# Output stores and turned transfers move one place back in the DMA queue, and the output tile gets six buffers

## Chip, cores and metric

The kernel runs on one core of one Trainium2 chip. The metric is device time in microseconds (us), the median of several runs.

## What is computed

Two layers in a row: attention with a relative position bias, and a mixture of eight low-rank adapters on its output.

```python
# q, k, v: (8 batches, 8 heads, 576, 64); bias_table: (32, 8)
scores = q @ k.T / sqrt(64) + bias_table[bucket(|i - j|)]   # per head
attn   = exp(scores - max) / (sum + 1e-9)
x      = (attn @ v)  ->  (4608 rows, 512)                   # heads side by side
logits = x @ w_gate                                         # 8 experts
topk   = the two largest; w = softmax over the two
out    = x + sum over the two of w_e * (x @ A[e]) @ B[e]    # A: 512x16, B: 16x512
```

Each batch gives 576 output rows: 512 from the main part and 64 from the tail.

## The kernel before, in words

**The pairs.** The work goes in 32 steps, one for each pair of heads of a batch: `u` counts them, batch `b = u // 4`, pair `hp = u % 4` (loop at L747). The order of the instructions on each engine is the order of the code, written out by hand. A pair's step has these parts:

- At the top, the SyncE queue issues loads: the tail of the next batch when `hp` is 0 (L754), `q` and `k` of pair `u + 4` (L758) and `v` of pair `u + 3` (L763). That is five loads a pair: one of `q`, two of `k`, two of `v`, 256 KB for each of the three.
- GpSimd casts `q` and `k` of pair `u + 2` and `v` of pair `u` to bf16 (`prep`, L722, with the casts at L137 and L141) and multiplies edge terms (L430, L432).
- TensorE makes four score tiles (`keys`, L368: L376 and L381) and ScalarE takes the exponential of each (L387), plus one for the edges of the next pair (L424). There are three score tiles in PSUM.
- TensorE multiplies the probabilities of the pair before with its values (L440, L450, L464), and VectorE divides by the sums (L508, L521). The results go to `xn`, and to `xe` for the 64 tail rows of two batches.
- TensorE transposes `q` and `k` of the next pair (L317), and VectorE copies the result (L321).

**The adapters.** Their work on a finished batch is spread over the next pairs by `moe` (L634), which enters each part in tables by pair number; the loop runs each table's entries at its place. A batch has two groups of two tiles of 128 rows, and each two batches have a group of one tile for the tail rows (`group`, L608). A group's parts, in order:

- Its rows have to be turned (transposed) into `xT`. Some tiles go through TensorE (L348, with a copy at L352; from batch 5 on L317 also), and the others through a turned transfer of the DMA, issued from SyncE: `send_x` (L355, issue at L357). The tables `send` and `sendx` hold these; `send` is run in the middle of a pair (L819), `sendx` at its end (L868). There are nine such transfers, and two more for the last batch (`send_last`, L360). `xT` has four buffers.
- Two to five pairs later, the gate matmuls read `xT` (`moe_z`, L539, matmul at L541), inside the group of matmuls of the values.
- Gate values follow on VectorE, ScalarE and GpSimd (L555 to L578), and a transposition on TensorE (L586).
- `moe_d` (L591) multiplies by `B` (L593) and adds `x` on VectorE into the tile `ot` (L596). `ot` belongs to the pool `ms`, which has three buffers for each tag. Each group has one buffer of two tiles, and each tile is stored as soon as it is done (L617, or L605 for tail rows). `moe_d` runs from the tables `dl2` (L816, L827) and `dls` (L847).

**The queue.** Nearly all DMAs are issued by SyncE, one after another: a transfer whose data is not ready holds all behind it. So the order in which the code issues loads, turned transfers and stores is the order in which they start. In the kernel before, a pair's queue is: loads, then the stores and turned transfers that come up in that pair.

**The end.** After the last pair, the last batch's adapters run by themselves (from L902), with their own stores (L1079, L1082, L1009).

Of the kernel before, what the change touches and what calls it, by code (L numbers as in the profile page):

```python
# [10 lines left out]
FP32 = mybir.dt.float32  # L11
# [26 lines left out]
def kernel(  # L38
# [14 lines left out]
    Dm = H * D  # L53
# [21 lines left out]
    ms = ctx.enter_context(tc.tile_pool(name="moe_sb", bufs=3))  # L75
# [15 lines left out]
    NU = len(units)  # L91
# [11 lines left out]
    def load(u, names="qkv", eng=nc.sync):  # L103
        b, hp = units[u]
        for nm in names:
            src = {"q": q, "k": k, "v": v}[nm]
            t = stg.tile([128, 2, 4 * D], FP32, name=f"{nm}s", tag=f"{nm}s")
            heads = src[b, 2 * hp:2 * hp + 2, :SM, :]
            if nm != "q":
                for h in range(2):  # L110
                    eng.dma_start(out=t[:, h, :].rearrange("p (g x) -> p g x", g=2),
                                      in_=heads[h].rearrange("(g p c) d -> p g (c d)", g=2, c=2))
            else:
                eng.dma_start(out=t, in_=heads.rearrange("h (p c) d -> p h (c d)", c=4))
            stage[(u, nm)] = t
# [425 lines left out]
            nc.tensor.matmul(zl, lhsT=gr.xT[:, t, c, :], rhs=AW[:, c, :], start=(first and c == 0),  # L541
                             stop=(c == 3), skip_group_check=True)

    left = []

    def moe_zc(gr, t, zl):
        if gr.z is None:
# [43 lines left out]
    def moe_d(gr, t):  # L591
        dl = mp.tile([128, Dm], FP32, name="dl", tag="mm")
        nc.tensor.matmul(dl, lhsT=gr.zT[:, t, :], rhs=Bc, start=True, stop=True)  # L593
        if gr.ot is None:
            gr.ot = ms.tile([128, len(gr.x), Dm], FP32, name="ot", tag="ot")
        nc.vector.tensor_tensor(gr.ot[:, t, :], dl, gr.x[t], op=ALU.add)  # L596
        gr.left -= 1
        if gr.solo:
            gr.store(gr.ot[:, t:t + 1, :], t)
        elif not gr.left:  # L600
            gr.store(gr.ot)

    def store_tail(b, ot, engs=(nc.sync, nc.sync)):
        for o in range(2):
            engs[o].dma_start(out=out[(b + o) * S + SM:(b + o + 1) * S, :],  # L605
                              in_=ot[64 * o:64 * o + 64, :])

    def group(b, i):  # L608
        gr = Group()
        gr.zT_ps, gr.z, gr.zT, gr.ot, gr.solo = {}, None, None, None, False  # L610
        if i < 2:
            gr.x = [xs[b][:, c, :] for c in (2 * i, 2 * i + 1)]
            gr.flat = xs[b][:, 2 * i:2 * i + 2, :].rearrange("p c d -> p (c d)")

            def store(ot, t=0):
                c, n = TILES[2 * i + t], ot.shape[1]
                nc.sync.dma_start(out=out[b * S:b * S + SM, :].rearrange("(p c) n -> p c n", c=4)  # L617
                                  [:, c:c + 2 * n - 1:2, :], in_=ot)
        else:
            gr.x = [xe[b // 2]]  # L620
            gr.flat = xe[b // 2]

            def store(ot, t=0):
                store_tail(b - 1, ot[:, 0, :])
        gr.store, gr.left = store, len(gr.x)
        return gr

    gate1, gates, xts, zs, zts, dls, send, sendx, xas, dl2 = ({} for _ in range(10))

    def at(where, u, *item):  # L630
        where.setdefault(u, []).append(item)


    def moe(b, u):  # L634
        g0, g1 = group(b, 0), group(b, 1)
        tiles = ((g0, 0), (g0, 1), (g1, 0), (g1, 1))
        k = B - 3 - b
        odd = b % 2
        for i in range(1 if odd else 3):
            if k >= 0:  # L640
                at(xas, u + 1 + i, *tiles[i])
        if k < 0:
            for i in range(4):
                at(xts, u + i // 2, *tiles[i])
        else:
            if k == 0:
                at(xts, u + 1, *tiles[1])
            elif odd:
                at(send, u, send_x, g0, 1, 2)
            at(sendx, u, send_x, g1, 1 - odd, 2)  # L650
        uz = (2, 3, 4, 5) if k > 0 else (2, 2, 3, 3) if k == 0 else (1, 1, 2, 2)
        ug, ut = ((5, 6), (6, 7, 8, 9)) if k > 1 else ((4, 6), (5, 6, 7, 8)) if k > 0 else ((3, 4), (4, 5, 5, 6)) if k == 0 else \
            ((2, 3), (3, None, None, None))
        ud = ((dls, 6), (dls, 7), (dls, 8), (dl2 if k == 2 else dls, 9)) if k > 1 else \
            ((dls, 5), (dls, 6), (dls, 7), (dls, 8)) if k > 0 else \
            ((dl2, 5), (dls, 5), (dl2, 6), (dls, 6)) if k == 0 else ((dls, 3),)
        for i, (g, t) in enumerate(tiles):
            at(zs, u + uz[i], g, t)
            if ut[i] is None:
                left.append((g, t))  # L660
            else:
                at(zts, u + ut[i], g, t)
                at(ud[i][0], u + ud[i][1], moe_d, g, t)
        for i, g in enumerate((g0, g1)):
            at(gate1, u + ug[i], moe_w, g)
            g.late = u + ug[i] - 1 if k > 1 and not i else None
            g.solo = True
        if b % 2:
            gt = group(b, 2)
            o = k == 0  # L670
            if o:
                at(send, u + 1, send_x, gt, 0, 1)
            else:
                at(xas, u + 2, gt, 0)
            w = 3 if k > 1 else o
            gt.late = u + 3 + w if k > 1 else None
            at(zs, u + 3 + o, gt, 0)
            at(gate1, u + 4 + w, moe_w, gt)
            at(zts, u + 5 + w + (k > 1) + (k == 2), gt, 0)
            at(dl2, u + 6 + w + (k > 1), moe_d, gt, 0)  # L680
# [6 lines left out]
    t = Turn()  # L687
# [14 lines left out]
    t = Turn()  # L702
# [38 lines left out]
    def run(items):  # L741
        for fn, *args in items:
            fn(*args)
# [3 lines left out]
    for u in range(NU):  # L747
# [12 lines left out]
            load_tail(1)  # L760
        if u + 3 < NU:
            load(u + 3, "v")
        for c in KO[:2]:  # L763
            keys(u, c)
            keys_exp(u, c)
# [12 lines left out]
        if u:  # L778
            pa = pva.pop(u - 2, None)
            oa = 256 if xa or hp == 0 else (ER + E) * (len(zb) > 1)  # L780
            ia = (XO - oa) // 64

            def bank_b():
                pv = values_b(u - 1)
                zl = pv[:, 260:260 + ER + E]
                for gr, t in zb[:1]:
                    moe_z(gr, t, zl, False)
                o = 260 + (ER + E) * bool(zb)
                for i, (gr, t) in enumerate(ta[ia:]):
                    moe_t(gr, t, pv, o + i * 64)  # L790
                return pv, zl

            if pa is not None:
                for gr, t in xa:
                    turn_x(gr, t, pa)
                values_x(u - 2, pa)
                for i, (gr, t) in enumerate(ta[:ia]):
                    moe_t(gr, t, pa, oa + 64 * i)
                za = pa[:, :ER + E]
                for gr, t in zb[1:]:  # L800
                    moe_z(gr, t, za, True)
                for gr, t in xa:
                    copy_x(gr, t)
                for gr, t in ta[:ia]:
                    moe_tc(gr, t)
                normalise_x(u - 2, pa)
                for gr, t in zb[1:]:
                    moe_zc(gr, t, za)
            pv, zl = bank_b()
            for gr, t in ta[ia:]:  # L810
                moe_tc(gr, t)
            normalise_b(u - 1)
            for gr, t in zb[:1]:
                moe_zc(gr, t, zl)
            if u < 16:
                run(dl2.pop(u, []))  # L816
            if hp == 0:
                corners(pa[:, :256], b)
            run(send.pop(u, []))  # L819
        else:  # L820
            t = Turn()
            turn_tail(t, 0, 2)
            copy_tail(t, 0, 2)
            corners(mp.tile([128, 256], FP32, name="cps", tag="mm"), 0)
# [3 lines left out]
        if 0 < u < NU - 1:  # L828
            t = Turn()
# [9 lines left out]
            if xt:  # L839
                gr, c = xt[0]  # L840
# [4 lines left out]
        keys(u, KO[3])  # L845
        keys_exp(u, KO[3])
        run(dls.pop(u, []))  # L847
        if u in (4, 5):
            weights_turn(u - 4)
        if u == 0:  # L850
            factors_l()
            factors_t()
            corners_bias(0)
            edge_bias(0)
            prep(0)
        else:
            if hp == 0:
                corners_bias(b)
            values_a(u - 1)
            if u == NU - 1:  # L860
                values_x(u - 1, pva[u - 1])
            normalise_a(u - 1)
            if u == NU - 1:
                normalise_x(u - 1, pva[u - 1])
            for gr, i in zb:
                at(gates, gr.late or u, moe_g, gr, i)
            run(gates.pop(u, []))
            run(sendx.pop(u, []))  # L868
        if u < 3:
            cast(u + 2, "q", nc.vector)  # L870
        if u == 3:
# [251 lines left out]
```

## Time and profile before

| | us |
|---|---|
| median of 3 runs | 197.11 |
| lowest and highest | 196.76, 197.35 |
| the profiled execution | 194.04 |
| its span in the profile | 192.2 |
| ScalarE busy | 166.0 |
| TensorE busy | 167.9 |
| GpSimd busy | 138.5 |
| VectorE busy | 135.3 |

The span is the time from the first to the last instruction that the profiler has; the rest of the execution's time lies around it. TensorE's busy time says less than the others', because matmuls are pipelined and their ends are modelled. In the profile, PE is TensorE, DVE VectorE, ACT ScalarE, POOL GpSimd and SP SyncE; SPq is SyncE's sequencer, which issues DMAs. A row in a timeline has the start, the duration, the engine, the line, what is written and read, and in brackets the idle time of the engine just before it and what ended that. A row xN joins N instructions. The chain of waits has a start, a duration, and the work or the DMA that ended last at that point.

### The profile page before, as it was taken

To read this page: it belongs to the slowest core of one execution; us is meant where nothing else is said; L and a number is where in the kernel's file an instruction comes from. 1 tells how busy PE (TensorE), PEld (TensorE's weight loads), DVE (VectorE), ACT (ScalarE), POOL (GpSimd) and SP (SyncE) were. 2 spreads that over 40 slices of the span, in tenths; PEclk is the share of its full clock that TensorE was granted. 3 is DMA by queue.
4 is the path that set the end of the run, shared out by engine and by line. 5 is a ranking of instruction groups with operands and counts; after the bars stand their busy time and mean duration, and the time that the engine had idled before them with its cause. 6 is when DMAs were issued, how large, how long until landed. Compare 5 with 4: busy or idle time off the path is not lost.

```text
span 192.2 us, 11327 instructions
## 1 busy us (share of the span) xinstructions
PE 167.9 (87%) x4834; PEld 122.4 (64%) x4834; DVE 135.3 (70%) x460; ACT 166.0 (86%) x206; POOL 138.5 (72%) x286
## 2 busy tenths in 40 slices
PE   0458799999999998999999999997999939999970
PEld 0345466777777776777776777775766737766840
DVE  4510457666658976999799779997799657988760
ACT  3159999999999999999999999999889956899680
POOL 5195859877986998599979986696798959636030
PEclk9999999999999999999999999999999978999998
DMA  5689989897877898898789975967999999334366
GB/s 148 192 186 263 295 209 254 238 216 175 246 180 187 227 283 230 241 226 247 238 233 188 306 229 161 256 155 239 282 235 256 205 279 258 132 98 143 113 234 204
DMA packets 72046, 41.77 MB, mean 217 GB/s; under 512 B 25772, under 2 KB 67252, under 8 KB 71996
## 3 DMA queue, kind: packets, MB, share of 16 engines
q1 hardware_dynamic: 71084, 40.58, 79.2%
q8 instruction: 37, 0.61, 1.3%
q10 hardware_dynamic: 912, 0.48, 1.0%
q14 instruction: 13, 0.11, 0.2%
HBM read 29.67 MB, written 9.47 MB: 204 GB/s over the span
## 4 chain that ended last, share of the span: by engine, by line
PE 59%; DVE 11%; ACT 11%; DMA 10%; issue 3%; POOL 3%; ACTq 0%; DVEq 0%; POOLq 0%
PE sc L376 13%; PE pv L440 13%; ACT pk L387 9%; PE sc L381 6%; DMA out_dram<-ot 5%; PE pv L464 4%; PE dl L593 4%; PE tp L317 4%; PE pv L541 3%; PE pv L450 3%; PE sc L417 3%; DMA Wt<-g_d 2%; DVE ot L596 2%; PE pv L348 2%; PE sc L422 1%
## 5 line engine op out<-in xcount | busy, mean ns | idle before, releaser
L387 ACT ACTIVATE pk<-sc 128x1024 bf16<-128x1024 f32 x128 | 124.1, 1032 | 2.8 <-PE sc L381 2.3
L376 PE MATMUL sc<-qkT 64*64 64x512 bf16 x512 | 52.8, 395 | 2.2 <-ACT pk L387 1.5
L381 PE MATMUL sc<-Wt,antw 64*64 64x384 bf16 (+1 forms) x512 | 44.4, 301 | 1.3 <-DMA Wt<-g_d 1.3
L440 PEld LDWEIGHTS <-pk 128*128 128x128 bf16 x1024 | 39.7, 98 | 6.1 <-issue 2.6
L440 PE MATMUL pv<-v,pk 128*128 128x65 bf16 x992 | 42.6, 194 | 0.4 <-POOL v L137 0.4
L424 ACT ACTIVATE pt<-sc 128x1024 bf16<-128x1024 f32 x32 | 32.8, 1025 | 9.0 <-PE sc L422 6.9
L321 DVE COPY qkT<-tp 128x1024 bf16<-128x1024 bf16 x32 | 22.0, 689 | 6.6 <-PE tp L317 5.7
L508 DVE TENSOR_TENSOR xn<-pv,rc 128x256 bf16<-128x256 f32 x56 | 23.8, 424 | 1.9
L376 PEld LDWEIGHTS <-qkT 64*64 64x64 bf16 x512 | 18.5, 107 | 10.3 <-issue 4.1
L432 POOL TENSOR_TENSOR pt<-pt,ET 64x256 bf16<-64x256 bf16 x32 | 21.3, 667 | 2.5
L141 POOL CAST kn<-ks 128x512 bf16<-128x512 f32 x30 | 18.4, 613 | 5.5 <-DMA ks<-in_k_dram 4.0
L137 POOL CAST v<-vs 128x512 bf16<-128x512 f32 x32 | 19.9, 621 | 0.1
L141 POOL CAST qn<-qs 128x512 bf16<-128x512 f32 x27 | 16.6, 616 | 4.5 <-DMA qs<-in_q_dram 3.2
L596 DVE TENSOR_TENSOR ot<-dl,xn 128x512 f32<-128x512 f32 x25 | 17.1, 685 | 3.9 <-DMA out_dram<-ot 3.2
L381 PEld LDWEIGHTS <-antw 64*64 64x64 bf16 x512 | 18.0, 109 | 1.9 <-issue 1.9
L450 PE MATMUL pv<-vb,pt 128*128 128x130 bf16 x124 | 17.4, 222 | 1.5 <-POOL pt L430 1.4
L464 PE MATMUL pv<-v,pt 128*128 128x65 bf16 x248 | 13.3, 196 | 3.5 <-DVE xn L508 3.3
L464 PEld LDWEIGHTS <-pt 128*128 128x128 bf16 x256 | 10.9, 99 | 8.4 <-issue 8.1
L317 PE MATMUL tp<-ident,qn 64*64 64x64 bf16 x512 | 11.6, 196 | 5.0 <-ACT qn L141 5.0
L317 PEld LDWEIGHTS <-qn 64*64 64x64 bf16 x512 | 10.7, 111 | 8.2 <-ACT qn L141 5.0
L430 POOL TENSOR_TENSOR pt<-pt,ELC 128x128 bf16<-128x128 bf16 x32 | 13.6, 425 | 1.3 <-ACT pt L424 0.6
L404 POOL TENSOR_TENSOR pc<-pcx,ELC 64x256 bf16<-64x256 bf16 x16 | 10.6, 665 | 4.4 <-ACT ELC L248 1.8
(144 smaller groups left out, 310.6 us busy)
## 6 DMA issues: line engine op xcount, KB each, us to landing
qs<-in_q_dram SPq DMA_DIRECT2D x32, 256.0 KB, 4.1
vs<-in_v_dram SPq DMA_DIRECT2D x64, 128.0 KB, 3.9
ks<-in_k_dram SPq DMA_DIRECT2D x62, 128.0 KB, 4.2
out_dram<-ot SPq DMA_DIRECT2D x25, 256.0 KB, 4.0
vt<-in_v_dram SPq DMA_DIRECT2D x8, 128.0 KB, 4.3
out_dram<-fot SPq DMA_DIRECT2D x4, 256.0 KB, 2.3
qkt<-in_q_dram SPq DMA_DIRECT2D x7, 128.0 KB, 4.6
qkt<-in_k_dram SPq DMA_DIRECT2D x7, 128.0 KB, 3.4
```

The source lines that it names most:

```text
L141: copy(t.rearrange("p c h d -> p h c d"), s)
L317: nc.tensor.transpose(self.ps[h * 64:h * 64 + 64, f, x * 64:x * 64 + 64], src[rows, h * 64:h * 64 + 64], ident[rows, rows])
L321: nc.vector.tensor_copy(_ap(dst, 0, [[64, 2], [128, n], [1, 64]]), self.ps[:, :, x * 64:(x + n) * 64].rearrange("p f (x t) -> p f x t", t=64))
L376: nc.tensor.matmul(sc[prt, h, :], lhsT=kT[rows, c * 128 + f * 64:c * 128 + f * 64 + 64], rhs=qT[rows, :], start=True, stop=False, skip_gro ...
L381: nc.tensor.matmul(_ap(sc[prt, h, :], p0, [[128, 4], [1, n]]), lhsT=turned_w(h), rhs=_ap(Wt[rows, hp, :], (1 - e) * GY + y0, [[GY, 4], [1, ...
L387: nc.scalar.activation(probs[u][0][c], scs.pop(c), ACT.Exp, scale=scale)
L424: nc.scalar.activation(probs[u][1][:, 64:], sc.rearrange("p h x -> p (h x)"), ACT.Exp, scale=scale)
L432: eng.tensor_tensor(te, te, ET[64:, :, hp, :], op=ALU.mult)
L440: nc.tensor.matmul(pv[:, o + h * W1:o + (h + 1) * W1], lhsT=pk[c][:, h, t * 128:(t + 1) * 128], rhs=vm[:, c, h, :], start=(first and h == ...
L450: nc.tensor.matmul(_ap(pv, o + h * W1, [[130, n], [1, W1]]), lhsT=pt[:, x0:x0 + 128], rhs=tvs[b % 2][:, t // 2:t // 2 + n, 2 * hp + h, :], ...
L464: nc.tensor.matmul(pv[:, o + h * W1:o + (h + 1) * W1], lhsT=src[:, x0:x0 + 128], rhs=rhs, start=(first and h == 0), stop=False, skip_group ...
L508: nc.vector.tensor_tensor(dst, _ap(pv, 0, [[2 * W1, 2], [W1, 2], [1, D]]), _ap(rc, i, [[2, 2], [1, 2], [0, D]]), op=ALU.mult)
```

## The change

Stores of `ot` and turned transfers by `send_x` are no longer issued where they come up. They are put in a list, `queued`, and issued at the top of the next pair, after that pair's loads. The list keeps their order. In the last pair it is run once more, behind the output additions; the two `send_last` transfers of pairs 30 and 31 are issued at once, as before. Each tile of `ot` is stored by itself, as it was for the two-tile groups; a one-tile group's store is the same either way. The tag `ot` has six buffers. The transfers' number and sizes stay, as do the instructions of all other engines and their order.

```diff
--- before.py
+++ after.py
@@ -541,7 +541,7 @@
             nc.tensor.matmul(zl, lhsT=gr.xT[:, t, c, :], rhs=AW[:, c, :], start=(first and c == 0),
                              stop=(c == 3), skip_group_check=True)
 
-    left = []
+    left, queued = [], []
 
     def moe_zc(gr, t, zl):
         if gr.z is None:
@@ -592,13 +592,10 @@
         dl = mp.tile([128, Dm], FP32, name="dl", tag="mm")
         nc.tensor.matmul(dl, lhsT=gr.zT[:, t, :], rhs=Bc, start=True, stop=True)
         if gr.ot is None:
-            gr.ot = ms.tile([128, len(gr.x), Dm], FP32, name="ot", tag="ot")
+            gr.ot = ms.tile([128, len(gr.x), Dm], FP32, name="ot", tag="ot", bufs=6)
         nc.vector.tensor_tensor(gr.ot[:, t, :], dl, gr.x[t], op=ALU.add)
         gr.left -= 1
-        if gr.solo:
-            gr.store(gr.ot[:, t:t + 1, :], t)
-        elif not gr.left:
-            gr.store(gr.ot)
+        queued.append((gr.store, gr.ot[:, t:t + 1, :], t))
 
     def store_tail(b, ot, engs=(nc.sync, nc.sync)):
         for o in range(2):
@@ -607,7 +604,7 @@
 
     def group(b, i):
         gr = Group()
-        gr.zT_ps, gr.z, gr.zT, gr.ot, gr.solo = {}, None, None, None, False
+        gr.zT_ps, gr.z, gr.zT, gr.ot = {}, None, None, None
         if i < 2:
             gr.x = [xs[b][:, c, :] for c in (2 * i, 2 * i + 1)]
             gr.flat = xs[b][:, 2 * i:2 * i + 2, :].rearrange("p c d -> p (c d)")
@@ -664,7 +661,6 @@
         for i, g in enumerate((g0, g1)):
             at(gate1, u + ug[i], moe_w, g)
             g.late = u + ug[i] - 1 if k > 1 and not i else None
-            g.solo = True
         if b % 2:
             gt = group(b, 2)
             o = k == 0
@@ -760,6 +756,8 @@
             load_tail(1)
         if u + 3 < NU:
             load(u + 3, "v")
+        run(queued)
+        queued.clear()
         for c in KO[:2]:
             keys(u, c)
             keys_exp(u, c)
@@ -816,7 +814,7 @@
                 run(dl2.pop(u, []))
             if hp == 0:
                 corners(pa[:, :256], b)
-            run(send.pop(u, []))
+            (queued.extend if u < NU - 2 else run)(send.pop(u, []))
         else:
             t = Turn()
             turn_tail(t, 0, 2)
@@ -845,6 +843,8 @@
         keys(u, KO[3])
         keys_exp(u, KO[3])
         run(dls.pop(u, []))
+        if u == NU - 1:
+            run(queued)
         if u in (4, 5):
             weights_turn(u - 4)
         if u == 0:
@@ -865,7 +865,7 @@
             for gr, i in zb:
                 at(gates, gr.late or u, moe_g, gr, i)
             run(gates.pop(u, []))
-            run(sendx.pop(u, []))
+            queued.extend(sendx.pop(u, []))
         if u < 3:
             cast(u + 2, "q", nc.vector)
         if u == 3:
```

## The prediction

> **What bounds the kernel now.** Read first, on the page, which engine is busiest, then the windows cut at the first exponential of each pair, which show where that engine loses time.
>
> ```profile
> PE 167.9 (87%) x4834; PEld 122.4 (64%) x4834; DVE 135.3 (70%) x460; ACT 166.0 (86%) x206; POOL 138.5 (72%) x286
> core 0: us, PE busy (x) PEld busy (x) DVE busy (x) ACT busy (x) POOL busy (x), PEclk, DMA share, GB/s
> 112.69:132.30 19.61, 19.59 (x584) 14.56 (x581) 17.65 (x61) 19.25 (x25) 13.70 (x27) 1.00 0.71 198
> 132.30:138.32 6.02, 4.95 (x146) 3.58 (x143) 3.82 (x13) 5.27 (x8) 4.63 (x12) 1.00 0.89 267
> 138.32:143.94 5.62, 5.55 (x166) 3.76 (x163) 4.76 (x17) 4.90 (x6) 5.26 (x10) 1.00 0.94 243
> 143.94:149.23 5.29, 5.29 (x149) 3.62 (x146) 5.05 (x19) 4.93 (x8) 4.47 (x10) 1.00 1.09 256
> 149.23:154.13 4.90, 4.57 (x149) 3.40 (x146) 3.04 (x11) 4.78 (x7) 4.58 (x10) 1.00 0.96 203
> 154.13:163.54 9.41, 6.40 (x183) 5.16 (x183) 6.02 (x22) 5.45 (x9) 6.93 (x14) 0.82 0.94 271
> ```
>
> Pairs 20 to 23 (first window) take 19.61 / 4 = 4.90 us each, and ScalarE is busy in 19.25 of the 19.61: the exponentials set the pace. Pairs 24, 25 and 26 take 6.02, 5.62 and 5.29 us, 2.23 us over three times 4.90. Pair 28 takes 9.41 us with ScalarE busy for 5.45. So the loss sits between 132 and 164 us, most of it in one pair. The chain of waits and VectorE's timeline say what happens there; the bracket is the idle time before an instruction and what ended it.
>
> ```profile
> 150.68 4.90 DMA out_dram<-ot
> 155.67 0.69 DVE ot L596
> ...
> 155.67 0.69 DVE L596 TENSOR_TENSOR ot<-dl,xn 128x512 f32<-128x512 f32 x1 [3.15 <-DMA out_dram<-ot]
> ```
>
> VectorE stood still for 3.15 us because all three `ot` buffers were taken: the oldest one's store was issued only at 150.68 and landed 4.90 us later. Why so late? SyncE's own timeline (start, duration, x count; `q` marks the issuing sequencer):
>
> ```profile
> 143.19 0.41 SPq L617 DMA_DIRECT2D out_dram<-ot  x1
> 143.71 1.91 SPq L357 DMA_TRANSPOSE xT<-xn  x1
> 145.68 0.57 SPq L114 DMA_DIRECT2D qs<-in_q_dram  x1
> 146.30 0.97 SPq L111 DMA_DIRECT2D ks<-in_k_dram  x2
> 147.37 0.93 SPq L111 DMA_DIRECT2D vs<-in_v_dram  x2
> 148.40 2.18 SPq L357 DMA_TRANSPOSE xT<-xe  x1
> 150.68 1.02 SPq L617 DMA_DIRECT2D out_dram<-ot  x2
> 151.75 0.44 SPq L114 DMA_DIRECT2D qs<-in_q_dram  x1
> 152.25 1.88 SPq L111 DMA_DIRECT2D ks<-in_k_dram  x2
> 154.22 0.93 SPq L111 DMA_DIRECT2D vs<-in_v_dram  x2
> 155.24 1.17 SPq L605 DMA_DIRECT2D out_dram<-ot  x2
> ```
>
> There is hardly a gap from row to row: SyncE issues without a pause and is behind. The loads issued at 145.68 are those that the code puts at the top of pair 25, and pair 25 began at 138.32 (the window's edge): 7.4 us late. So the order on this queue decides when each thing lands. I take it that the same list of issues, permuted, reaches the same point at the same time; that is the main assumption.
>
> **The change part by part.** Instructions on TensorE, VectorE, ScalarE and GpSimd stay the same, in the same order. Only SyncE's order changes (each store and turned transfer goes behind the next pair's five loads), and `ot` has six buffers in place of three.
>
> *Six buffers.* No instruction is added. The wait of 3.15 us goes: minus 3.15. Stores landing some 3 us later cannot bring it back, since a buffer is now reused after six groups and not three. What is late next is worked out below.
>
> *Loads earlier.* Each load moves ahead of what is put behind it. The loads of 151.75 move up by the two stores and the transfer of 148.40: 151.75 - 148.40 = 3.35 us. GpSimd's cast waited for them:
>
> ```profile
> 156.76 0.61 POOL L141 CAST qn<-qs 128x512 bf16<-128x512 f32 x1 [1.76 <-DMA qs<-in_q_dram]
> ```
>
> 3.35 is over 1.76, so that wait goes. Such waits are part of the 2.23 us of pairs 24 to 26; between 0 and 2.23 comes back there. I price it at nothing in the sum, because the next step holds pair 27 by the clock of SyncE, however early the pair is ready.
>
> *Turned transfers later.* This is the change's cost. The gate matmuls (L541) read `xT`, and TensorE runs in order. Rows of `xT`'s tile view and of TensorE's timeline:
>
> ```profile
> DMA to landing us min/median/max: 3.8/4.3/4.9
> 149.21 0.40 PE L541 MATMUL pv<-AW,xT 128*128 128x136 bf16 x4
> 150.65 0.33 PE L381 MATMUL sc<-Wt,antw 64*64 64x256 bf16 x4
> 151.94 0.68 PE L440 MATMUL pv<-v,pk 128*128 128x65 bf16 x16
> 156.96 0.60 PE L464 MATMUL pv<-v,pt 128*128 128x65 bf16 x8 [3.17 <-DVE xn L508]
> 157.57 1.09 PE L440 MATMUL pv<-v,pk 128*128 128x65 bf16 x16
> 158.67 0.66 PE L541 MATMUL pv<-AW,xT 128*128 128x136 bf16 x4
> ```
>
> The transfer of 143.71 (batch 5, second group) is read at 149.21, in pair 27; 143.71 + 4.3 = 148.0, so it has 1.2 us to spare. After the change, the slot at 143.19 holds the five loads (148.40 - 145.68 = 2.72 us), then the store (0.52), then the transfer: it starts at 146.43 and lands at 150.7 (150.2 to 151.3). The matmul waits until then, 1.5 us beyond its time now. Queued behind it on TensorE are the second gate matmul, the value matmuls and the third score tile, whose exponentials wait. Now that tile is done at 150.65 + 0.33, 1.77 after 149.21; then it is 150.7 + 1.77 = 152.5. Its exponential started at
>
> ```profile
> 151.14 1.95 ACT L387 ACTIVATE pk<-sc 128x1024 bf16<-128x1024 f32 x2
> ...
> 160.34 1.99 ACT L387 ACTIVATE pk<-sc 128x1024 bf16<-128x1024 f32 x2
> ```
>
> so ScalarE is put back by 152.5 - 151.1 = 1.4 us, say 1.3, as the pieces behind it may run closer: plus 1.3, and pair 28 begins that much later.
>
> The transfer of `xe` (148.40 now): the first transfer's end is 146.43 + 1.97 = 148.40, then five loads (155.24 - 151.75 = 3.49): start 151.89, landing 156.2 (155.7 to 156.8). Its reader stands at 158.67; without the 3.15 and with the 1.3 it is due at 156.8. It just fits: 0, at worst some 0.4.
>
> Earlier transfers have room. The tightest:
>
> ```profile
> 58.87 3.63 SPq L357 DMA_TRANSPOSE xT<-xn  x2
> 62.55 0.58 SPq L114 DMA_DIRECT2D qs<-in_q_dram  x1
> ...
> 65.93 0.47 SPq L114 DMA_DIRECT2D qs<-in_q_dram  x1
> ...
> 68.71 0.40 PE L541 MATMUL pv<-AW,xT 128*128 128x136 bf16 x4
> ```
>
> The first of the two would start at 58.87 + 3.38 = 62.25 and land by 67.2 at 4.9, and is read at 68.71: nothing.
>
> *Clock.* In the window of pair 28 the granted clock is 0.82, and the sixteen value matmuls took 1.09 us at 157.57 against 0.68 at 151.94. A pause of 3.17 us precedes them. With that pause gone and the new one about 1.5 to 3 us, I count the 0.41 of this one group: minus 0.4. Between 0 and, were the new pause to bring the low clock into pair 27, plus 0.4.
>
> [...]
>
> *Stores later.* From pair 29 on there are no loads left, and the queue has the old order. The store lines add or drop no issue. Nothing.
>
> [...]
>
> **Sum:** -3.15 + 1.3 - 0.4 = -2.25, taken as 2.2 us. Against the profiled execution's own 194.04 that is 191.8. The median of the runs shown is 197.11, 3.07 above it; the same step gives **194.9 us**. If the unprofiled runs are longer because their queue is slower, gain and loss both grow, so I widen the range a little.
>
> **Rivals.**
>
> *A. The transfers come too late (slower).* Place: TensorE's L541 in pair 27, and the one of `xe` in pair 28. Every us that they land later than worked out costs a us. The point from which it decides is 2.2 us: landing after 152.9 and 158.4. For it: issue rows vary without a cause that I can name:
>
> ```profile
> 115.58 2.74 SPq L129 DMA_DIRECT2D qkt<-in_q_dram  x1
> ```
>
> where its neighbours in kind take about 0.6, and a transfer itself took 1.91 in one row and 2.18 in another. One such stall (+2.1), a landing of 4.9 (+0.6) and a low clock (+0.8 against the sum) make +3.5: net 1.3 slower, 198.4. Against it: all must fall on the same five loads.
>
> *B. The queue gets ahead.* If the stores and transfers hold the queue by their waits for data, loads run ahead early, everything is issued at least 3 us sooner by pair 25, and `xT` is in time. Then -3.15 - 0.4 and about half of the 2.23: -4.7, 192.4. Against it: the rows shown have no gaps, and data of a pair 7 us back is long there.
>
> *C. No difference.* The transfers take back just what the buffers give: landings about 1.6 to 2.8 us later than worked out. Within 0.6 us of 197.1. Pair 28 has 6.02 us of VectorE work, so the pair will not be short in any case.
>
> **How the numbers follow.** About 0.3% (0.6 us) is what can be told from no change here. Chances: forecast 0.58, A 0.17, B 0.13, C 0.12. The forecast's own range, from landings 150.2 to 151.3, `xe`'s 0.4 and the clock's two ends, is 193.9 to 196.1. The 8-in-10 range takes in most of B below and C and the milder half of A above: 192.6 to 197.5. Faster: 0.58 + 0.13 = 0.71, of which 0.01 is given to same; same 0.13; slower 0.17, which leaves faster at 0.70.
>
> **What would show it.** Right: no VectorE wait on `out_dram<-ot`; a TensorE wait at L541 on `xT<-xn` near 150 us; the q cast near 153 without a wait; pair 28 about 6 us long. Wrong: SyncE reaching the transfers at another time than 146.4 and 151.9 (the assumption of equal pace), L541 waiting in other pairs, or another engine stopping VectorE in pair 28.

## The result, and the profile after

The changed kernel is slower by about 1%: 198.95 us (median of 22 executions, 195.88 to 204.70) against 197.23 us for the kernel before (22 executions, 194.49 to 201.66), a ratio of 1.0127 with a 95% interval of 1.008 to 1.0175. The forecast was 194.9 us and a range of 192.6 to 197.5. The ratios here and below leave out executions that lie over 1.5% above the fastest of their kernel, so medians, which hold all of them, stand beside them.

The profiled execution of the changed kernel took 201.67 us, with a span of 199.9. It lies above its median by 2.7, as that of the kernel before lay 3.2 below its own. So the two traces are compared place by place and not by their totals; later a second trace of each checks what is read here.

First the page: busy times, then the groups of the gate matmuls and of the addition into `ot` (busy time, mean ns of one, idle time before and what ended it).

```profile
PE 169.9 (85%) x4833; PEld 122.6 (61%) x4834; DVE 135.0 (68%) x460; ACT 166.3 (83%) x206; POOL 139.1 (70%) x286
...
L387 ACT ACTIVATE pk<-sc 128x1024 bf16<-128x1024 f32 x128 | 124.3, 1030 | 12.5 <-PE sc L381 11.9
...
L541 PE MATMUL pv<-AW,xT 128*128 128x136 bf16 x124 | 12.6, 226 | 6.0 <-DMA xT<-xn 6.0
L596 DVE TENSOR_TENSOR ot<-dl,xn 128x512 f32<-128x512 f32 x25 | 17.1, 686 | 0.6 <-PE dl L593 0.2
```

VectorE's wait for an `ot` buffer is gone (0.6 us idle, none of it for the store). In its place TensorE waits 6.0 us for `xT`, and ScalarE stands idle 11.9 us for score tiles (2.3 in the kernel before). The windows by pair tell where; the first is pairs 20 to 23, the others are pairs 24 to 28:

```profile
core 0: us, PE busy (x) PEld busy (x) DVE busy (x) ACT busy (x) POOL busy (x), PEclk, DMA share, GB/s
116.49:136.15 19.66, 19.55 (x580) 14.46 (x577) 17.00 (x62) 19.26 (x26) 15.30 (x31) 1.00 0.89 228
136.15:141.08 4.93, 4.93 (x148) 3.62 (x145) 3.71 (x13) 4.93 (x9) 2.99 (x6) 1.00 0.85 257
141.08:147.57 6.49, 5.66 (x167) 3.89 (x165) 4.78 (x16) 4.92 (x7) 5.98 (x13) 1.00 0.91 231
147.57:152.89 5.32, 5.32 (x149) 3.64 (x145) 5.06 (x18) 4.97 (x7) 4.01 (x9) 1.00 1.03 280
152.89:164.06 11.17, 6.50 (x161) 4.81 (x159) 4.61 (x19) 5.00 (x7) 7.70 (x15) 0.85 1.15 220
164.06:170.26 6.20, 4.53 (x162) 3.32 (x159) 4.19 (x15) 5.33 (x8) 3.65 (x8) 1.00 0.77 236
```

Pair 28 took 6.20 us in place of 9.41: the 3.2 that the buffers were to give did come. But pair 27 took 11.17 in place of 4.91, 6.26 more. TensorE's and ScalarE's timelines inside it:

```profile
152.83 0.23 PE L586 MATMUL pv<-ident,zt 128*128 128x128 bf16 x1
157.73 0.41 PE L541 MATMUL pv<-AW,xT 128*128 128x136 bf16 x4 [4.67 <-DMA xT<-xn]
157.97 1.04 PE L440 MATMUL pv<-v,pk 128*128 128x65 bf16 x16
...
161.87 0.68 PE L440 MATMUL pv<-v,pk 128*128 128x65 bf16 x16
```

```profile
160.69 2.17 ACT L387 ACTIVATE pk<-sc 128x1024 bf16<-128x1024 f32 x2 [5.76 <-PE sc L381]
```

4.67 of the 6.26 is the wait for the turned transfer of batch 5's second group. Behind it a group of sixteen matmuls takes 1.04 us, and a like group 0.68 four us later: the granted clock is 0.85 on average in that window, and 0.50 in the 3.41 us from 158.01. ScalarE is thus put back by 5.76. SyncE's timeline and the chain of waits show the transfer itself:

```profile
147.29 1.25 SPq L614 DMA_DIRECT2D out_dram<-ot  x1
148.59 0.43 SPq L114 DMA_DIRECT2D qs<-in_q_dram  x1
149.07 1.02 SPq L111 DMA_DIRECT2D ks<-in_k_dram  x2
150.19 0.93 SPq L111 DMA_DIRECT2D vs<-in_v_dram  x2
151.22 0.41 SPq L614 DMA_DIRECT2D out_dram<-ot  x1
151.74 1.50 SPq L357 DMA_TRANSPOSE xT<-xn  x1
```

```profile
151.74 5.95 DMA xT<-xn
```

The order is as foreseen: five loads, a store, the transfer, 3.15 us from the first load to the transfer (3.24 in the forecast). But pair 25's loads were issued at 148.59, 7.51 us after the pair began at 141.08, and the transfer took 5.95 us to land, not 4.3. A second, smaller wait of the same kind stands in pair 19, where the kernel before had none:

```profile
112.43 0.41 PE L541 MATMUL pv<-AW,xT 128*128 128x136 bf16 x4 [1.34 <-DMA xT<-xn]
```

Its transfer in SyncE's timeline, in the kernel before and in the changed one, where pair 19 began at 107.78 and at 110.08:

```profile
98.83 1.75 SPq L357 DMA_TRANSPOSE xT<-xn  x1
```

```profile
108.14 1.22 SPq L357 DMA_TRANSPOSE xT<-xn  x1
```

The two spans differ by some 7.6 us. Pairs 27 and 28 together make 3.05 of it and pair 19 1.5; the rest lies over many pairs, and a part of it comes by TensorE's instructions, which are the subject of the later experiments.

### The profile page after: what moved, and what is told of

It reads as the page before. It is cut to its first block, busy times and chain, and to the rows that moved or that the text cites. A ratio compares the mean times of both kernels' runs of the same rounds, so it can differ in the third digit from the quotient of the medians.

```text
span 199.9 us, 11323 instructions
## 1 busy us (share of the span) xinstructions
PE 169.9 (85%) x4833; PEld 122.6 (61%) x4834; DVE 135.0 (68%) x460; ACT 166.3 (83%) x206; POOL 139.1 (70%) x286
## 4 chain that ended last, share of the span: by engine, by line
PE 63%; DMA 12%; ACT 9%; DVE 7%; issue 4%; POOL 3%; ACTq 0%; POOLq 0%; DVEq 0%
PE sc L376 14%; PE pv L440 13%; PE sc L381 7%; ACT pk L387 7%; DMA xT<-xn 5%; PE tp L317 5%; PE dl L593 4%; PE pv L464 4%; PE pv L541 3%; PE sc L417 3%; PE pv L450 3%; DMA Wt<-g_d 2%; PE pv L348 2%; DMA out_dram<-ot 2%; PE sc L422 2%
## 5 line engine op out<-in xcount | busy, mean ns | idle before, releaser
L387 ACT ACTIVATE pk<-sc 128x1024 bf16<-128x1024 f32 x128 | 124.3, 1030 | 12.5 <-PE sc L381 11.9
L376 PE MATMUL sc<-qkT 64*64 64x512 bf16 x512 | 54.0, 400 | 2.2 <-ACT pt L424 0.8
L381 PE MATMUL sc<-Wt,antw 64*64 64x384 bf16 (+1 forms) x512 | 45.3, 304 | 1.3 <-DMA Wt<-g_d 1.1
L376 PEld LDWEIGHTS <-qkT 64*64 64x64 bf16 x512 | 18.4, 108 | 11.9 <-issue 5.9
L141 POOL CAST qn<-qs 128x512 bf16<-128x512 f32 x27 | 16.6, 614 | 6.6 <-DMA qs<-in_q_dram 2.8
L541 PE MATMUL pv<-AW,xT 128*128 128x136 bf16 x124 | 12.6, 226 | 6.0 <-DMA xT<-xn 6.0
L317 PE MATMUL tp<-ident,qn 64*64 64x64 bf16 x512 | 11.7, 198 | 5.2 <-ACT qn L141 5.2
L589 DVE COPY zT<-pv 128x128 bf16<-128x128 bf16 x28 | 5.9, 220 | 11.3 <-PE pv L541 7.9
```

What stands on the lines that cost most here:

```text
L141: copy(t.rearrange("p c h d -> p h c d"), s)
L317: nc.tensor.transpose(self.ps[h * 64:h * 64 + 64, f, x * 64:x * 64 + 64], src[rows, h * 64:h * 64 + 64], ident[rows, rows])
L376: nc.tensor.matmul(sc[prt, h, :], lhsT=kT[rows, c * 128 + f * 64:c * 128 + f * 64 + 64], rhs=qT[rows, :], start=True, stop=False, skip_gro ...
L381: nc.tensor.matmul(_ap(sc[prt, h, :], p0, [[128, 4], [1, n]]), lhsT=turned_w(h), rhs=_ap(Wt[rows, hp, :], (1 - e) * GY + y0, [[GY, 4], [1, ...
L387: nc.scalar.activation(probs[u][0][c], scs.pop(c), ACT.Exp, scale=scale)
```

## The experiments

All are compared with executions of the kernel before on the same chip. The ratio has its 95% interval.

| kernel | median us (executions) | before, same chip | ratio |
|---|---|---|---|
| e1 six buffers only | 198.03 (12) | 197.47 (23) | 0.9998 (0.9893 to 1.0103) |
| e2 transfers later only | 200.42 (12) | 197.47 | 1.0157 (0.9977 to 1.0338) |
| e3 stores later, six buffers | 195.78 (6) | 197.47 | 0.9835 (0.9738 to 0.9932) |
| e4 changed, last two transfers in place | 196.40 (6) | 197.47 | 0.9842 (0.9764 to 0.9921) |
| e5 e3, one transfer later | 200.69 (12) | 200.11 (30) | 1.0071 (0.9989 to 1.0153) |
| e6 changed, three loads a pair | 199.81 (7) | 200.11 | 1.0172 (1.0099 to 1.0246) |
| e7 changed, longer pieces | 199.68 (12) | 200.11 | 1.0012 (0.9914 to 1.0110) |
| e8 changed, half of each store | 199.94 (12) | 200.11 | 1.0005 (0.9888 to 1.0121) |
| e9 the changed kernel again | 203.12 (6) | 198.83 (18) | 1.0196 (1.0056 to 1.0337) |
| e10 the kernel before again | 198.80 (1) | 198.83 | |
| e11 changed, v loaded once | 191.57 (6) | 198.83 | 0.9748 (0.9684 to 0.9813) |
| e12 e3 again | 198.60 (13) | 198.83 | 1.0050 (0.9989 to 1.0111) |
| e13 before, bias matmuls left out | 196.26 (6) | 199.83 (11) | none (one execution far below the rest) |
| e14 e4 again | 198.33 (6) | 199.83 | 0.9894 (0.9769 to 1.0018) |
| e15 changed, all loads once | 189.91 (6) | 199.83 | 0.9603 (0.9550 to 0.9656) |
| e16 changed, bias matmuls left out | 196.78 (6) | 199.83 | 0.9897 (0.9804 to 0.9989) |

### The parts of the change: e1 to e4

e1 is the kernel before with

```diff
-            gr.ot = ms.tile([128, len(gr.x), Dm], FP32, name="ot", tag="ot")
+            gr.ot = ms.tile([128, len(gr.x), Dm], FP32, name="ot", tag="ot", bufs=6)
```

> Theory L (the turned transfers' later landing is what costs; the buffers by themselves help): VectorE's wait of 3.15 us for out_dram<-ot in pair 28 goes, L541 waits no more than before, and pair 28 falls from 9.4 to about 6 us: 2 to 3.5 us faster than before, ratio 0.983 to 0.990. Rival S (putting work on the queue in another order does nothing, and the wait for the buffer only hides another wait in pair 28): ratio 0.997 to 1.003, with another engine named in pair 28.

The wait on `ot` went, and no gain is seen: 0.9998, the time that rival S gave, with an interval of 1% to each side. Pair 28 fell to 5.62 us, but just behind it, in GpSimd's timeline, the cast of q waits for a load, and pair 29 took 11.04 us (5.71 in the kernel before):

```profile
161.60 0.61 POOL L141 CAST qn<-qs 128x512 bf16<-128x512 f32 x1 [4.25 <-DMA qs<-in_q_dram]
```

So in this trace a late load took the place of the late store.

e2 is the changed kernel with three buffers and the stores at once:

```diff
-        queued.append((gr.store, gr.ot[:, t:t + 1, :], t))
+        gr.store(gr.ot[:, t:t + 1, :], t)
```

> Only the turned transfers are issued behind the next pair's loads; stores stand where they were, with three buffers. Theory L: L541 waits on xT<-xn in pair 27 for 2 to 5 us, and the wait for the ot buffer in pair 28 is partly covered by it: 1 to 5 us slower than before, ratio 1.005 to 1.025. Rival T (late stores are what makes the changed kernel slow, not the transfers): ratio 0.997 to 1.003, with no wait at L541.

e3 is the other half, the changed kernel with the transfers in their old places:

```diff
-            (queued.extend if u < NU - 2 else run)(send.pop(u, []))
+            run(send.pop(u, []))
...
-            queued.extend(sendx.pop(u, []))
+            run(sendx.pop(u, []))
```

> Stores behind the next pair's loads and six buffers, turned transfers where they were before. Theory L: no wait for ot, no wait at L541 over 0.5 us, loads earlier by a store: 2.5 to 4.5 us faster than before, ratio 0.977 to 0.988, and not slower than six buffers alone. Rival T: the late stores slow it, ratio 1.005 or more.

e4 is the changed kernel with `queued.extend` only for `u < 24` in both lines, so that batch 5's transfers are issued at once.

> The changed kernel, but the turned transfers of pairs 24 and 25 (batch 5) are issued at once, as before; the other seven stay behind the loads. Theory L, if the cost is at pair 27 alone: 3.5 to 6 us faster than the changed kernel, 1 to 4 us faster than before (ratio to before 0.980 to 0.995). If the transfers of pairs 8 and 16 cost as well, 1 to 2 us of waits at L541 stay in pairs 8 to 19 and the ratio is 0.990 to 1.000. Rival T: as slow as the changed kernel, ratio 1.010 to 1.015.

e2 has the long pair 27 (10.14 us, 3.28 of it the wait at L541); e3 and e4 have no wait over 0.3 us there, and pair 27 takes 4.90 and 5.23. So the wait comes with the transfers and not with the stores or buffers. How much e3 and e4 gain was not settled by one chip; see e12 and e14.

### When the transfer is late: e5 and e9

e5 is e3 with one transfer put later, that of pair 24: `(queued.extend if u == 24 else run)(sendx.pop(u, []))`.

> The kernel with the stores later and six buffers (e3, 0.984 of the kernel before), and of the nine turned transfers only one later: that of batch 5's second group (table sendx, pair 24). Theory T (this one transfer is the whole loss, because its slack is under the five loads and one store it is put behind): TensorE waits 1 to 5 us at L541 on xT in pair 27, and the time comes back up to 1.00 to 1.02 of before. Rival A (the loss is the sum of many small delays over all nine transfers, or lies with the transfer of xe): a wait under 1 us at that place and 0.98 to 0.99 of before, like e3 and e4.

There was no wait at L541 in pair 27 in its trace (the pair took 4.90 us), against theory T as it was stated. But in this execution the queue was not late: pair 25's loads were issued 1.26 us after the pair began. So the condition was missing from the theory, and e9, the changed kernel unaltered, was to try it. e5's time, 1.0071, lies in theory T's range all the same; its trace is of an execution of 197.86 us, below its median of 200.69, and what the longer ones had in pair 27 is not shown.

> The changed kernel itself, a second execution with a trace. Theory T (in this order the turned transfer of batch 5 is late whenever the queue is 5 us or more behind its pair, whatever made it late): TensorE waits again at L541 in pair 27, 2 to 6 us if pair 25's loads are issued 5 us or more after the pair began, and under 1 us if they are not. Rival (that wait was an accident of one execution): none of 1 us or more though the queue is late. Time 1.005 to 1.02 of before.

```profile
159.36 0.41 PE L541 MATMUL pv<-AW,xT 128*128 128x136 bf16 x4 [4.41 <-DMA xT<-xn]
```

The wait came again, 4.41 us, with the queue 5.56 us late; pair 27 took 10.90 us and pair 19 waited 1.44. The places of this one transfer in all the traces but that of e15 (us, worked out from SyncE's rows and the starts of the pairs, as above; "in place" as in the kernel before):

| kernel | transfer | pair 25's loads late by | transfer issued, from pair 25's start | to landing | wait in pair 27 |
|---|---|---|---|---|---|
| before, e10 | in place | 7.35, 9.75 | 5.39, 8.34 | 4.51, 4.53 | 0, 0.70 |
| e1, e13 | in place | 8.71, 8.24 | 7.32, 5.29 | 3.22, 5.73 | 0, 0 |
| e3, e12 | in place | 7.53, 5.63 | 4.40, 4.23 | 5.64, 5.61 | 0, 0 |
| e4, e14 | in place | 4.31, 8.34 | 2.93, 6.25 | 5.76, 4.88 | 0, 0 |
| changed, e9 | behind loads | 7.51, 5.56 | 10.66, 9.46 | 5.95, 5.76 | 4.67, 4.41 |
| e2 | behind loads | 6.28 | 9.75 | 5.28 | 3.28 |
| e8 | behind loads | 8.52 | 11.71 | 5.79 | 4.76 |
| e16 | behind loads | 4.68 | 8.99 | 4.81 | 3.18 |
| e5, e7 | behind loads | 1.26, 0.59 | 5.44, 4.65 | 4.47, 5.35 | 0, 0 |
| e6, e11 | behind loads | -5.53, -6.08 | -1.18, -0.90 | 5.59, 4.67 | 0, 0 |

All five with the transfer behind the loads and the queue 4.7 us or more late wait 3.2 to 4.8 us; with it in place no trace waits over 0.7; with a punctual queue it does not matter. That settles the mechanism of this wait. Both traces of the changed kernel are of executions above its medians (201.67 against 198.95, 204.30 against 203.12), so how often the shorter ones have the wait is not shown; e16's trace, with a wait of 3.18, is of an execution at its median (196.66 against 196.78).

### What holds the queue: e6, e7, e8 and e11

e6 loads k and v of a pair with one DMA each, in q's row order:

```diff
-                for h in range(2):
-                    eng.dma_start(out=t[:, h, :].rearrange("p (g x) -> p g x", g=2),
-                                      in_=heads[h].rearrange("(g p c) d -> p g (c d)", g=2, c=2))
+                eng.dma_start(out=t, in_=heads.rearrange("h (p c) d -> p h (c d)", c=4))
```

> The changed kernel, but k and v of a pair are each loaded by one DMA in q's row order in place of two (three loads a pair in place of five, the same bytes in pieces of 1 KB in place of 512 B); the rows of k and v stand in another order than the bias table's, so this changes what is computed, not how much. Theory I (the queue is bound by the number of issues): two issues of some 0.5 us a pair are saved, the queue is no longer 6 to 8 us behind its pair but under 4, the transfer of batch 5 is in time, 0.97 to 0.98 of before. Theory B (it is bound by the bytes that the 16 engines move): the same bytes, so the queue is as late as in the changed kernel, and the time 1.00 to 1.02 of before.

e7 keeps two DMAs for each, with the same longer pieces: `eng.dma_start(out=t[:, h, :], in_=heads[h].rearrange("(p c) d -> p (c d)", c=4))`.

> The changed kernel with five loads a pair as before, but k and v in pieces of 1 KB (q's row order within a head) in place of 512 B; again the order of rows, not the amount, is changed. It parts the two edits of e6. If the number of issues decides (theory I): as the changed kernel, 1.00 to 1.02 of before, and e6 faster than this by 2 us or more. If the size of the pieces decides (theory P): as e6, 0.97 to 0.98. If only bytes count (theory B): e6, e7 and the changed kernel all alike.

e8 stores half the columns: `[:, c:c + 2 * n - 1:2, :256], in_=ot[:, :, :256]`.

> The changed kernel, but the stores of tiles of 128 rows inside the loop write only the first 256 of 512 columns (the other half of these rows of the output is left unwritten): the same number of issues, some 3.2 MB less of 41.8 MB. Theory B (bytes): 3.2 MB at about 240 GB/s is 13 us of the queue's time by the end of the loop, of which some 10 by pair 25: the queue catches up, no wait at L541, 0.97 to 0.98 of before. Theory I (issues): no change of the queue, the wait at L541 of 2 to 5 us stays, 1.00 to 1.02 of before.

On the queue theory I held for two of the three: with three loads a pair it runs ahead (pair 24's loads were issued 3.7 us before the pair began), while with half the store bytes it is as late as ever (9.91 and 8.52 us at pairs 24 and 25), with the wait of 4.76 at L541. e7 does not fit it: with five issues and longer pieces the queue was only 3.18 and 0.59 late there, and nothing waited for `xT`. Whether the pieces did that or this execution is not shown, since e5, with the old pieces, was 2.41 and 1.26 late. On the time no theory held throughout: theory I's ranges hold for e7 and e8 (1.0012 and 1.0005) and not for e6, whose 1.0172 is the worst of the three and lies in theory B's range. Not one of these kernels is faster than the kernel before. In e6's trace, which is of its longest execution (205.06 us), TensorE stands still with no releaser ("issue"), and the page's chain gives 8% of the span to that, 4% in the changed kernel:

```profile
34.57 0.39 PE L438 MATMUL pv<-v,pk 128*128 128x65 bf16 x7 [0.84 <-issue]
...
81.72 0.22 PE L315 MATMUL tp<-ident,kn 64*64 64x64 bf16 x2 [0.67 <-issue]
...
164.57 0.26 PE L315 MATMUL tp<-ident,kn 64*64 64x64 bf16 x8 [2.10 <-issue]
```

The same instruction shows in other traces: the last two of one pair's transposes, in the changed kernel and in e5.

```profile
76.83 0.22 PE L317 MATMUL tp<-ident,kn 64*64 64x64 bf16 x2 [0.67 <-issue]
```

```profile
77.31 0.22 PE L317 MATMUL tp<-ident,kn 64*64 64x64 bf16 x2 [1.88 <-issue]
```

Counted through TensorE's stream of matmuls and weight loads, the gaps over 0.6 us that nothing ends stand, in every trace of this study and without exception, at the same remainder of the count by 256. The page has a DMA queue that fits (packets, MB, share of 16 engines):

```profile
q8 instruction: 37, 0.61, 1.4%
```

0.61 MB / 37 = 16 KB a packet, and 9667 instructions of TensorE / 256 = 38. A gap ends 1.2 to 1.8 us after a packet's end, with three exceptions among some 125. So TensorE's instructions come in blocks of 256 over the same DMA engines, and a late block stops it. Counted from the start of one instruction to the start of the next, the gaps at these places (from 0.3 us each) add up to 0.8 us in the kernel before, 6.5 in the changed one, 11.7 in e7 and 17.7 in e6.

e11 was to tell whether a queue that runs ahead makes the packets late, or the data. It loads v once:

```diff
+            if nm == "v" and u > 4:
+                stage[(u, nm)] = stage[(4, nm)]
+                continue
+            pool = cp if nm == "v" and u == 4 else stg
-            t = stg.tile([128, 2, 4 * D], FP32, name=f"{nm}s", tag=f"{nm}s")
+            t = pool.tile([128, 2, 4 * D], FP32, name=f"{nm}s", tag=f"{nm}s")
```

> The changed kernel, but v is loaded once (pair 4) and all later pairs cast that one tile: 54 DMAs and 6.9 MB fewer, so what is computed for v is wrong data; every other instruction stays. The queue is surely ahead then, as in e6, with a fifth less data. Theory Q (the lateness of the queue is what costs time, here and before): no waits for loads, xT or ot, 0.95 to 0.965 of before. Theory F (a queue that runs ahead fills the DMA engines, the instruction packets come late and TensorE stalls): stalls of 8 us or more as in e6, 0.985 to 1.01. If the stalls go by the amount of data alone: under 3 us, and the time of theory Q.

0.9748, with 3.0 us of gaps though the queue ran 4 to 6 us ahead. So running ahead does not by itself make the packets late. It fell short of theory Q's 0.965 all the same.

### Is it the change, or the execution: e10 and e12

> The kernel before itself, a second execution with a trace, for the spread of its own parts. TensorE's stream is fetched in packets of 16 KB, one for 256 of its instructions, and in the traces so far TensorE stands still at every 256th instruction where such a packet starts late: 0.75 us in all in the first trace of this kernel, 5.8 in that of the changed one, 17.7 with three loads a pair. Theory F (these stalls are a part of what the order of the loads changes): under 3 us here again. Rival (they differ from execution to execution whatever the kernel): 4 us or more in this one. VectorE's wait on the store of ot in pair 28: 2 to 4 us by the first trace.

> The kernel of e3 (stores later and six buffers, turned transfers in their old place), on the same chip as the changed kernel. Theory T: no wait of 1 us or more at L541, and faster than e9 by 1.5 to 3%, so 0.98 to 0.995 of before. Rival (e3's gain was the luck of its few runs): as e9 or as the kernel before, 0.995 to 1.015.

The kernel before had 5.4 us of gaps in its second trace, so the rival held for them: they differ from execution to execution. Its wait on `ot` was there again, but shorter:

```profile
DVE ot L596 <- DMA out_dram<-ot: 2.3, 2, 2.1
POOL qn L141 <- DMA qs<-in_q_dram: 4.2, 3, 1.7
```

e12 was 1.0050 where the same kernel had been 0.9835: e3's gain did not repeat. Its trace, of its longest execution, had 13.1 us of gaps. Against e9 on the same chip e12 is 4.5 us faster by the medians; the two differ only in that e9 puts the transfers later.

### TensorE's instructions: e13, e16, e15, and e14

e13 is the kernel before, and e16 the changed kernel, without the bias matmuls from pair 1 on:

```diff
-                             rhs=qT[rows, :], start=True, stop=False, skip_group_check=True)
-        for rows, prt, h, f in halves:
+                             rhs=qT[rows, :], start=True, stop=True, skip_group_check=True)
+        for rows, prt, h, f in halves if u < 1 else ():
```

> The kernel before, without the bias matmuls of the score tiles from pair 1 on (L381 leaves the position bias out): 32 of some 300 TensorE instructions a pair go, nothing else. The DMA queue is the same. Theory F (TensorE needs 256 instructions in 4.4 us, and a packet of instructions that starts later than some 1.6 us after the last one was used up stops it; this costs each kernel 1 to 13 us and is the larger part of its scatter): a packet now serves 4.9 us, stalls under 1.5 us in all, 0.97 to 0.985 of before, with the waits for ot and for loads still there. Rival Q (the loads' queue alone sets the time; the stalls lie beside it): stalls gone, but the waits for ot, q and k grow by as much, 0.99 to 1.005.

> The changed kernel with the same matmuls left out as in e13. Theory T (the transfers put later cost some 4 to 6 us in pair 27, the buffers give back 2 to 3): 1 to 2.5% slower than e13, with a wait of 3 to 5 us at L541 in pair 27. If the change's loss came by the instruction packets and not by that wait: within 0.5% of e13.

The gaps were 0.7 and 1.5 us (0.8 and 5.4 in the two traces of the kernel before, 6.5 and 5.8 in those of the changed one), and e13's executions (191.97 to 196.63) all lie below those of the kernel before (196.80 to 203.50), 3.6 us by the medians. That this time is the gaps' is not shown: the pairs themselves are shorter without these matmuls. Pairs 14 and 15, which nothing disturbs, take 4.75 us each in e13 and 4.90 in the kernel before, and 0.1 to 0.15 us in each of 31 pairs is 3 to 4.6 us. The queue's waits stayed, as theory F had it: 3.66 us on `ot` in pair 28, and one on q:

```profile
DVE ot L596 <- DMA out_dram<-ot: 3.7, 1, 3.7
POOL qn L141 <- DMA qs<-in_q_dram: 6.6, 5, 3.4
```

e16 has the wait in pair 27 as expected, and another in pair 11:

```profile
70.81 0.41 PE L541 MATMUL pv<-AW,xT 128*128 128x136 bf16 x4 [1.70 <-DMA xT<-xn]
...
153.95 0.63 PE L541 MATMUL pv<-AW,xT 128*128 128x136 bf16 x4 [3.18 <-DMA xT<-xn]
```

But it was only 0.5 us slower than e13 (0.3%), not 1 to 2.5%: the time is the rival's (within 0.5%), though the wait that the rival left out is there. Pairs 27 and 28 took 9.32 + 5.56 = 14.88 us against 4.77 + 9.71 = 14.48: with a transfer that comes 0.5 to 1.7 us earlier after pair 25's start than in e9 and the changed kernel, and lands 1 us sooner, loss and gain nearly cancel. In the full kernel those pairs took 14.32 and 15.22 us (before, e10) and 17.37 and 16.30 (changed, e9).

e15 is e11's edit without its `nm == "v"`: no loads of q, k and v after pair 4.

> The changed kernel with q, k and v loaded for pairs 0 to 4 only; all later pairs cast pair 4's tiles (so wrong data in them): 134 DMAs and some 20 MB fewer. Theory F, its other side (data in flight is what delays the instruction packets): they start on average under 1.0 us after the last one was used up, in place of 1.3 to 2.6 in the traces so far, stalls under 1 us in all. Rival: the delay is the fetch's own, 1.3 us or more, stalls of 2 us or more, as with v alone loaded once (3.0). Both: no waits for loads, xT or ot, 0.94 to 0.965 of before.

The packets started 0.90 us on average after TensorE began the last instruction of the block before (1.30 and 1.55 in the two traces of the kernel before, 1.64 and 1.60 in those of the changed one, 1.36 in e11, 2.39 in e6), the gaps were 0.4 us, and the time 0.9603. So with most loads gone the packets come earlier, which is theory F's other side; e6, with all the bytes and the latest packets, shows that the amount of data alone does not set the delay.

> The kernel of e4 (the changed kernel, but the transfers of pairs 24 and 25 in their old place) on another chip. Theory T: no wait of 1 us or more at L541 in pair 27, one of some 1.4 us in pair 19 if the queue is late there; no gain left over the kernel before, since stores later and six buffers gave none on the second chip: 0.99 to 1.01. If e4's 0.984 was real: 0.98 to 0.99.

No wait in pair 27, one of 1.60 in pair 19, as theory T has it. The time, 0.9894 with an interval that reaches 1, lies at the edge between its range and that of a real gain. Both times (e4, e14) this version's median was below that of the kernel before, by 1.07 and 1.50 us. It is the best of those that keep the whole computation, by some 0.5 to 1.6%, with e3 close to it (1.69 us below the kernel before, and 0.23 in e12); these runs do not make the gain certain.

## Why the prediction was wrong, point by point

- **Six buffers, minus 3.15**: right at its place. The wait is gone and pair 28 took 6.20 us, as forecast. But the step did not ask what else is late while VectorE waits: in e1's trace loads took the place of the buffer, and the term by itself gained nothing there.
- **Loads earlier, nothing**: q's cast near 155 had no wait, as forecast. As a price it was sound, since pairs 24 to 26 took 16.74 us in place of 16.93.
- **Turned transfers later, plus 1.3: this is the step that failed.** Pair 27 cost 6.26 us more. The mechanism was the one described; the size was not. The forecast had the transfer landing 150.7 - 138.32 = 12.4 us after pair 25's start, and the reader due 10.9 after it. It landed 157.68 - 141.08 = 16.6 after it, and the reader was due (157.73 - 4.67 - 141.08) 12.0 after it. Of the 4.2 us, 2.6 are the queue: the loads were 7.51 us behind their pair where the permuted list would have put them 143.19 - 138.32 = 4.87 behind. 1.1 of that is pair 24, which ran in 4.93 us in place of 6.02 and left the queue behind; the rest is the queue itself, with longer rows such as a store of 1.25 us where 0.41 is usual. The other 1.65 are the landing. In e9 the same sum is 0.7 for the loads, 0.7 for longer rows up to the transfer and 1.5 for the landing: 15.2 after pair 25's start.
- **Equal pace** was therefore the wrong assumption, and in one more way: the queue's lead over the pairs differs from execution to execution (pair 25's loads were 1.3 to 9.75 us late with five loads of the old kind and all their data), so one trace could not give it to a microsecond.
- **Earlier transfers, nothing**: wrong for pair 19. The row of 58.87 was named as the tightest; the one that cost was another, which the kernel before issued at 98.83, 8.95 us before pair 19 began (107.78), and the changed kernel at 108.14, 1.94 before it (110.08). It cost 1.3 to 1.6 us in three traces (the changed kernel, e9, e14) and 0.56 in that of e8. The one named as the tightest cost nothing in these, and 1.70 in e16.
- **The transfer of `xe`, nothing**: right; no wait on it in the changed kernel.
- **Clock, minus 0.4**: wrong sign. The old pause of 3.17 went, but a new one of 4.67 came, and the low clock with it: the granted clock was 0.50 for 3.41 us in both kernels (from 156.39 in the kernel before, from 158.01 in the changed one), and pair 27's 6.26 is 4.67 and about 1.6 of what follows. The length of a pause alone does not tell whether that happens: the first sixteen value matmuls took 0.97 us behind a pause of 1.88 (e5), and 0.68, as in undisturbed pairs, behind one of 2.60 (e12).
- **Rival A** is what happened: its place (L541 in pair 27), its point of decision (2.2 us later than worked out; it was 4.2 and 2.8) and its price, 198.4 against 198.95. That the price is so near is partly luck: pair 19's wait, which rival A does not have, is in the measured time, and so is the scatter of the executions. It was given 0.17 on the ground that a stall, a late landing and a low clock must fall on the same five loads. They came together in both traces: 2.6 and 1.4 us of the queue, 1.65 and 1.5 of the landing, and the low clock, which came right behind the pause (0.50 from 158.01, 0.28 us after the pause ended; in e9 sixteen value matmuls took 0.95 us from 159.61, 0.25 after it ended).

What is still open: how much of the whole loss is this wait, since pairs 27 and 28 together cost 3.05 us between the first two traces and 1.08 between those of e9 and e10, while the medians differ by 1.7 and 4.3; why this transfer takes 5.3 to 6 us to land in some traces and 3.2 to 4.9 in others, and what makes the packets of instructions late in one execution and not in the next. That e6 delays them most, with as many bytes as e7, is not explained either.

## What to carry to other kernels

When a queue runs behind, an issue that is moved back starts behind the whole of what it is moved past, on top of the lateness that the queue happens to have (3.15 us on top of 7.51 in the changed kernel); price it from the reader's side (start, landing, due time) with the worst lateness that the trace shows, for every transfer that is moved and not only the nearest. A wait that is taken away on such a queue gives back only what no other late transfer takes (in e1 GpSimd then waited 4.25 us for a load of q): look for the next one in line before the gain is booked. And where executions of one kernel differ by more than the change is worth, take two traces of each before a term is read to the microsecond.

## What the runs showed of the hardware

- TensorE's instructions come by DMA in packets of 16 KB, one for 256 instructions (37 packets, 0.61 MB, for 9667 instructions), and TensorE used up 256 in about 4.5 us here. On average a packet started 0.9 us after TensorE began the last instruction of the block before with few loads in flight (e15) and 1.3 to 2.4 with all of them, and took 1.1 to 1.3 us; where TensorE stood still, it went on 1.2 to 1.8 us after the packet's end. By an estimate from these figures under 1 us is to spare with all the loads (4.5 less 1.3, 1.1 and 1.2 is 0.9). TensorE stood still at the edges of these blocks for 0.4 (e15) to 17.7 us (e6) in one execution. With 32 instructions fewer a pair (4.97 us for 256) it was 0.7 (e13) and 1.5 us (e16).
- Executions of the kernel before scattered from 192.3 to 205.3 us over all chips. On one chip eleven of them lay between 196.8 and 203.5, and six of e15, without most loads, between 188.8 and 190.6.
- Issuing a DMA took SyncE 0.4 to 0.65 us in 134 of the 208 rows of one issue in the first two traces, with 50 rows of 1 to 2.74 among them. With five loads a pair, those of pair 25 were up to 9.75 us late (e10), with three they were 5.53 us early (e6), and with half the bytes of the stores they were 8.52 us late (e8), 7.51 and 5.56 in the changed kernel.
